# A decode block on one core: short loops on every engine, a model dimension cut in four chunks of 112, and a TensorE program that is walked over once before it runs

## The chip, the cores and the metric

The kernel runs on one core of a Trainium2 chip. The metric is the device time in microseconds of that core, from launch to end; the kernel before has a median of 1302.09 us over 3 runs (1301.49 to 1303.19). The profiler gives one further execution, with the time of every instruction and of every DMA packet.

## The reference, cut to what matters

Everything is fp32. One token (Sq = 1) for B = 2 batches goes through one attention block over a cache of 8192 keys and values per head, and one gated feed-forward block.

```python
B, D, H, Sk, Dh, F = 2, 448, 16, 8192, 256, 1792
x = A_x                                             # [2, 1, 448]
q = (layernorm(x) @ wq).reshape(B, 1, H, Dh)        # wq [448, 4096]
scores = einsum("bhqd,bhkd->bhqk", q, k_cache) * Dh ** -0.5
o = einsum("bhqk,bhkd->bhqd", softmax(scores), v_cache)
h = x + o.reshape(B, 1, H * Dh) @ wo                # wo [4096, 448]
n = layernorm(h)
return h + ((n @ w_gate) * (n @ w_up)) @ w_down     # [448, 1792] twice, [1792, 448]
```

Keys and values are 2 x 16 x 8192 x 256 numbers each, 268 MB and 268 MB; the weights add 24 MB.

## The kernel before, in words

There are 32 pairs of head and batch, numbered i = 0 to 31 (`NQ`). For each pair, K(i) is one load of 8 MB into one of two SBUF buffers (`k_sb[i % 2]`, 128 partitions by 64 keys by 256) and V(i) one load of 8 MB into a single buffer `v_sb`. SP issues all loads but x, in the order of its program; its DMA queue works them off in that order. After K(0) and K(1) come V(0), K(2), V(1), K(3) and so on. SP waits before each: K(i+1) is issued when VectorE is done with K(i-1) (`m_in[i-1]`), V(i) when TensorE has mixed V(i-1) (`pe("M", i-1)`), and V(0), which lies where the weight wq lay, when all queries are projected (`all_q`).

VectorE multiplies K(i) in place with the query, spread over the 128 partitions (`score`, L334), and adds up each key's 256 products (L337): first the 16 keys per partition of `HC`, then the other 48. Between them it does small steps of the pair before (`neg_max` L343, `norm` L348). TensorE (`find_top` L422, `spread_top` L426, `add_up` L431, `spread_query` L270, `mix` L413, `turn_up` L438) finds the maximum, sums the exponentials, spreads the next query and mixes V(i) in 32 matmuls. ScalarE does the exponentials and the copies out of PSUM. An fp32 matmul stands in the profile as two MATMUL records and two LDWEIGHTS records.

Only TensorE's program has a loop, over 31 of the 32 pairs, in which its waits compare a semaphore with a number worked out from the loop's register (`emit_part`). VectorE, ScalarE and SP have every pair written out. After the loop TensorE's program goes on with the last pair, the output projection, and the feed-forward block.

The model dimension of 448 is cut as three chunks of 128 rows and one of 64. The 64 rows of the last chunk lie in two halves of the 128 partitions: its left columns on partitions 0 to 63, its right columns on partitions 64 to 127 (`pack`, `LAYOUT`). So wq, w_gate and w_up are loaded as 128 partitions of 3.5 x 4096, 3.5 x 1792 and 3.5 x 1792 numbers, with no hole. `LAYOUT` needs a fifth slot in `xz` and `xr`, filled with zeros where the other half's rows would be.

At the end, SP issues wo (two loads, behind `m_in[30]`), V(31) in two parts of 48 and 16 keys per partition (`LASTV`), wg (w_gate) and wu (w_up, two loads) behind `m_in[31]`, and wd (w_down, four loads of `DOWN` = 5, 5, 3 and 1 blocks) behind the mix of V(31)'s first part (`mixed_a`). The last steps are the matmuls with wd (L738), a copy (L747) and the store of the output.

Of the kernel before, what the change touches and what calls it, by code (L numbers as in the profile page):

```python
# [9 lines left out]
EPS = 1e-5  # L10
P = 128
HALF = 64
DC = 4
YN, YW = 4, D // 4
# [7 lines left out]
LASTV = 48  # L22

FG = (512, 512, 384, 384)
FO = (0, 512, 1024, 1408)
NF = F // P
FH = FG[0] // 2
WIDE = [[min(n, (k + 1) * FH) - k * FH for n in FG] for k in range(2)]
PACKED = [3 * sum(n) + n[0] + n[2] for n in WIDE]
# [3 lines left out]
LAYOUT = (  # L33
    (slice(0, P), slice(0, DC - 1), slice(0, DC - 1)),
    (slice(0, HALF), slice(DC - 1, DC), slice(DC - 1, DC)),
    (slice(HALF, P), slice(DC - 1, DC), slice(DC, DC + 1)),
)


class Line:  # L40


    def __init__(self, nc, engine, name):
        self.e = engine
        self.sem = nc.alloc_semaphore(name=name)
        self.n = 0
        self.seen = {}

    def wait(self, *tokens):
        for sem, n in tokens:  # L50
            if self.seen.get(sem.num, 0) < n:
                self.e.wait_ge(sem, n)
                self.seen[sem.num] = n

    def did(self, ins):
        ins.then_inc(self.sem, 1)
        self.n += 1
        return self.sem, self.n


class Tensor:


    def __init__(self, nc):
        self.e = nc.tensor
        self.sem = nc.alloc_semaphore(name="pe")
        self.n = 0
        self.parts = [(None, [])]

    def loop(self, *turns):  # L70

        self.parts.append((turns or None, []))

    def do(self, make, *waits, inc=False):
        self.parts[-1][1].append((make, waits, inc))
        if inc:
            self.n += 1
            return self.sem, self.n

    def emit(self):  # L80
        for turns, ops in self.parts:
            if turns:
                with self.e.Fori(*turns) as turn:
                    self.emit_part(ops, turn)
            else:
                self.emit_part(ops, None)

    def emit_part(self, ops, turn):
        seen = {}
        for make, waits, inc in ops:  # L90
            for w in waits:
                sem, n = w[:2]
                if len(w) == 3:
                    self.e.wait_ge(sem, turn * w[2] + n)
                elif seen.get(sem.num, 0) < n:
                    self.e.wait_ge(sem, n)
                    seen[sem.num] = n
            ins = make() if turn is None else make(turn)
            if inc:
                ins.then_inc(self.sem, 1)  # L100


def decode_block(nc, x, k_cache, v_cache, wq, wo, wg, wu, wd, out):
# [6 lines left out]
    bank = [nc.alloc_psum_tensor(f"bank{i}", [P, 512], F32)[:] for i in range(8)]  # L110
    first_sem = nc.alloc_semaphore(name="dve_first")
    V = Line(nc, nc.vector, "dve")
    A = Line(nc, nc.scalar, "act")
    A_q = Line(nc, nc.scalar, "act_q")
    G = Line(nc, nc.gpsimd, "pool")
    S = Line(nc, nc.sync, "sp")
    T = Tensor(nc)

# [3 lines left out]
    def load(line, dst, src, sem, n=16):  # L122
        line.e.dma_start(dst, src).then_inc(sem, 16)  # L123
        return sem, n
# [5 lines left out]

    room = {"at": 2 * NF * D}

    def late(*shape):

        n = 1
        for k in shape[1:]:
            n *= k
        at = room["at"]
        room["at"] += -(-n // 8) * 8
        assert room["at"] <= NJ * DH  # L140
        got = k_flat[1][: shape[0], at : at + n]
# [15 lines left out]
    xr = sb("xr", P, DC + 1, B, 16)  # L157
    xz = sb("xz", P, DC + 1, B)
    sel = sb("sel", P, 2)
    rep = sb("rep", P, 2, B, REP)  # L160
    q_sb = sb("q_all", B, H * DH)

    s_x, s_wq, s_k0 = landing("x"), landing("wq"), landing("k0")
    s_k = [landing("k_even"), landing("k_odd")]
    s_v, s_v2 = landing("v"), landing("v_last")
    s_wo = [landing("wo_a"), landing("wo_b")]
    s_wg, s_wu = landing("wg"), [landing("wu_a"), landing("wu_b")]
    s_wd = [landing(f"wd{i}") for i in range(len(DOWN))]
    s_out = landing("out")
# [7 lines left out]
    x_in = load(A, x_sb, x.rearrange("b s d -> (b s) d"), s_x)  # L177
    wq_t = v_flat[:, : 3 * H * DH + H * DH // 2]
    wq_in = load(S, wq_t, wq, s_wq)
    k0_in = load(S, k_sb[0][:, :HC], keys_of(k_cache, 0, 0, HC), s_k0)  # L180
    k_in = {0: load(S, k_sb[0][:, HC:], keys_of(k_cache, 0, HC, NJ), s_k[0])}
    k_in[1] = load(S, k_sb[1], keys_of(k_cache, 1, 0, NJ), s_k[1])

    zero = G.did(nc.gpsimd.memset(ident, 0.0))
    G.wait(zero)
    ident_in = G.did(
        nc.gpsimd.affine_select(
            out=ident, in_=ident, compare_op=ALU.not_equal, fill=1.0, base=0,
            pattern=[[-1, P]], channel_multiplier=1,
        )  # L190
    )
    G.did(nc.gpsimd.memset(xz, 0.0))
    zeros_in = G.did(nc.gpsimd.memset(xr[:, DC - 1 :], 0.0))

    V.did(nc.vector.memset(eps_t, EPS))
    V.did(nc.vector.memset(ones, 1.0))
    V.did(nc.vector.memset(avg, 1.0 / D))
    V.did(nc.vector.memset(row, DH**-0.5))
    o_ps, h_ps, y_ps = bank[0], bank[5][:, :P], bank[6][:, :YW]
    V.wait(x_in)  # L200
    xsum = sb("xsum", B, 1)
    t = V.did(nc.vector.tensor_reduce(xsum, x_sb, axis=AX.X, op=ALU.add))
    V.wait(t)
    xmean = sb("xmean", B, 1)
    t = V.did(nc.vector.tensor_scalar(xmean, xsum, -1.0 / D, None, op0=ALU.mult))
    V.wait(t)
    xc_sb = sb("xc", B, DC * P)
    t = V.did(nc.vector.tensor_scalar(xc_sb[:, :D], x_sb, xmean, None, op0=ALU.add))
    V.wait(t)
    xc_in = V.did(nc.vector.tensor_copy(xc_sb[:, D:], xc_sb[:, D - HALF : D]))  # L210
    xq = o_sb[:B, :D]
    t = V.did(nc.vector.tensor_mul(xq, xc_sb[:, :D], xc_sb[:, :D]))
    V.wait(t)
    xvar = sb("xvar", B, 1)
    var_in = V.did(nc.vector.tensor_reduce(xvar, xq, axis=AX.X, op=ALU.add))

    std = sb("std", B, 1)
    A.wait(var_in)
    std_in = A.did(nc.scalar.activation(std, xvar, AF.Sqrt, bias=eps_t, scale=1.0 / D))
    rstd = sb("rstd", B, 1)  # L220
    V.wait(std_in)
    rstd_in = V.did(nc.vector.reciprocal(rstd, std))
    A.wait(rstd_in)
    A.did(nc.scalar.activation(std, std, AF.Exp, scale=0.0))

    xT_ps = bank[3][:, : DC * B].rearrange("p (c b) -> p c b", b=B)
    for c in range(DC):
        xT_in = T.do(
            lambda c=c: nc.tensor.transpose(
                xT_ps[:, c, :], xc_sb[:, c * P : (c + 1) * P], ident[:B, :B]  # L230
            ),
            ident_in, xc_in, inc=c == DC - 1,
        )
    V.wait(xT_in, zeros_in)
    for rows, c, to in LAYOUT:
        xz_in = V.did(nc.vector.tensor_copy(xz[rows, to], xT_ps[rows, c]))

    V.wait(ident_in)
    V.did(
        nc.vector.tensor_reduce(  # L240
            sel, ident.rearrange("p (g r) -> p r g", r=32)[:, :2, :], axis=AX.X, op=ALU.add
        )
    )
    V.did(
        nc.vector.tensor_copy(
# [4 lines left out]
    for ps in (o_ps, h_ps, bank[4][:, :HW]):  # L250
        set_in = V.did(nc.vector.memset(ps, 0.0))

    q_sel = sb("q_sel", B, DH)
    qb = [sb(f"qb{i}", P, DH) for i in range(2)]
    qb_ps = bank[1][:, :DH]
    q_ps = [bank[7][:B, :], bank[4][:B, :]]
    qsel_in, qb_in, Q_in = {}, {}, {}

    def select(i):
        h, b = divmod(i % NQ, B)  # L260
        if i > 0:
            A.wait(Q_in[i - 1])
        qsel_in[i] = A_q.did(
            nc.scalar.activation(  # L264
                q_sel, q_sb[:, h * DH : (h + 1) * DH], AF.Copy, scale=ident[:B, b : b + 1]
            )
        )

    def spread_query(*_):
        return nc.tensor.matmul(qb_ps, ones[:B, :], q_sel, start=True, stop=True)  # L270

    def take_query(i):
        A.wait(Q_in[i])
        qb_in[i] = A_q.did(nc.scalar.activation(qb[i % 2], qb_ps, AF.Copy))  # L274

    q_in = {}
    for g in range(NG):
        for c in range(DC):
            xs = c if c < DC - 1 else c + g // (NG // 2)
            at = c * H * DH + (g * QG if c < DC - 1 else g % (NG // 2) * QG)  # L280
            done = T.do(
# [536 lines left out]
```

## Time and profile before

| what | before |
|---|---|
| median of 3 runs | 1302.09 us (1301.49 to 1303.19) |
| profiled execution, its own time | 1301.42 us |
| its span, first to last instruction | 1300.1 us |
| VectorE busy | 1131.2 us (87%) |
| TensorE matmuls busy | 470.6 us (36%) |
| ScalarE busy | 81.5 us (6%) |
| DMA from HBM | 561.19 MB, mean 432 GB/s over the span |
| share of the span in which the SP queue's packets keep 16 DMA engines | 99.7% |

The page gives busy time per engine, the span in 40 slices, the DMA queues, the chain of work that ended last, and the costliest groups of instructions. Busy shares say which engine could be the bound; the wait in front of an instruction, with what released it, says which is.

### The profile page before, as it was taken

The numbers are of one execution on the slowest core, as the hardware profiler recorded it, in microseconds if no ns is written. First come the engines' busy times: TensorE is split into PE (matmuls) and PEld (weight loads), VectorE is DVE, ScalarE is ACT, GpSimd is POOL, SyncE is SP. The second block draws the span as 40 slices with busy tenths as digits, with TensorE's granted clock in tenths as the row PEclk, the third lists the DMA queues.
The fourth block names the chain that finished last, engine by engine and source line by source line (L and its number), as shares of the span: only waits on it lengthen the run. The fifth ranks groups of instructions, "written<-read, shape, count | busy, mean of one in ns | idle before, by whom it ended". The sixth has DMA issues, their size and how long they took to land.

```text
span 1300.1 us, 6914 instructions
## 1 busy us (share of the span) xinstructions
PE 470.6 (36%) x2992; PEld 155.1 (12%) x2992; DVE 1131.2 (87%) x266; ACT 81.5 (6%) x239; POOL 0.8 (0%) x8
## 2 busy tenths in 40 slices
PE   3643224333323433322333322333321333432387
PEld 0111011101001101101101101101100110110123
DVE  1999998889888889888889988888988888988861
ACT  1100000000000000000000000000000000000000
POOL 0000000000000000000000000000000000000000
PEclk9866566666556666556666656666656666655689
DMA  9999999999999999999999999999999999999998
GB/s 411 427 450 421 450 421 444 426 436 436 421 450 421 448 423 448 423 446 425 442 427 427 444 421 450 422 446 425 446 423 446 425 440 429 427 444 423 446 421 367
DMA packets 10973, 561.31 MB, mean 432 GB/s; under 512 B 1234, under 2 KB 1364, under 8 KB 1492
## 3 DMA queue, kind: packets, MB, share of 16 engines
q1 hardware_dynamic: 10960, 561.19, 99.7%
q8 instruction: 5, 0.08, 0.0%
q14 instruction: 4, 0.03, 0.0%
q10 hardware_dynamic: 4, 0.00, 0.0%
HBM read 561.19 MB, written 0.00 MB: 432 GB/s over the span
## 4 chain that ended last, share of the span: by engine, by line
DMA 74%; PE 25%; issue 0%; ACT 0%; SPq 0%; DVE 0%
DMA v<-in_A_v_cache_dram 71%; PE bank L413 22%; PE bank L282 2%; DMA v<-in_wd_dram 2%; DMA v<-in_wq_dram 1%; PE bank L270 0%; SPq L123 0%; PE bank L738 0%; ACT q_all L290 0%; ACT q_sel L264 0%; DVE k L747 0%; ACT qb L274 0%
## 5 line engine op out<-in xcount | busy, mean ns | idle before, releaser
L334 DVE TENSOR_TENSOR k<-k,qb 128x4096 f32<-128x4096 f32 x64 | 555.3, 8676 | 124.2 <-DMA k<-in_A_k_cache_dram 95.9
L337 DVE TENSOR_REDUCE s<-k 128x16 f32<-128x4096 f32 x64 | 555.2, 8675 | 1.1
L413 PE MATMUL bank<-v,p 128*2 128x512 f32 x2048 | 291.4, 733 | 342.9 <-DMA v<-in_A_v_cache_dram 342.9
L413 PEld LDWEIGHTS bank<-v,p 128*2 128x2 f32 x2048 | 53.6, 96 | 573.4 <-DMA v<-in_A_v_cache_dram 365.9
L426 PE MATMUL bank<-nm,row 1*128 1x1 f32 x64 | 18.4, 354 | 227.6 <-DVE nm L343 227.6
L422 PE MATMUL bank<-ident,m 128*1 128x128 f32 x32 | 11.8, 368 | 184.4 <-DVE m L381 184.4
L363 ACT ACTIVATE o_sb<-bank 128x512 f32<-128x512 f32 x31 | 18.5, 597 | 604.0 <-PE bank L413 604.0
L426 PEld LDWEIGHTS bank<-nm,row 1*128 1x128 f32 x64 | 15.6, 302 | 236.9 <-DVE nm L343 236.9
L438 PE MATMUL bank<-sel,o_sb 128*128 128x1 f32 x256 | 33.7, 253 | 23.3 <-ACT o_sb L363 22.5
L270 PE MATMUL bank<-q_sel,ones 2*128 2x256 f32 x66 | 39.0, 691 | 1.4 <-ACT q_sel L264 1.4
L438 PEld LDWEIGHTS bank<-sel,o_sb 128*128 128x128 f32 x256 | 31.0, 191 | 53.1 <-ACT o_sb L363 51.5
L282 PE MATMUL bank<-v,xz 128*2 128x512 f32 x64 | 30.7, 639 | 16.0 <-DMA v<-in_wq_dram 16.0
L352 ACT ACTIVATE nb<-bank 128x1 f32<-128x1 f32 x32 | 5.5, 171 | 441.5 <-PE bank L426 441.5
L431 PE MATMUL bank<-lsum,ones 128*128 128x1 f32 x64 | 18.5, 359 | 23.5 <-ACT p L355 23.5
L422 PEld LDWEIGHTS bank<-ident,m 128*1 128x1 f32 x32 | 2.5, 79 | 188.2 <-DVE m L381 187.8
L431 PEld LDWEIGHTS bank<-lsum,ones 128*128 128x128 f32 x64 | 15.8, 306 | 26.2 <-ACT p L355 26.2
L270 PEld LDWEIGHTS bank<-q_sel,ones 2*128 2x128 f32 x66 | 15.9, 297 | 3.7 <-ACT q_sel L264 2.4
L264 ACT ACTIVATE q_sel<-q_all,ident 2x256 f32<-2x256 f32 x33 | 16.2, 492 | 0.0
L274 ACT ACTIVATE qb<-bank 128x256 f32<-128x256 f32 x32 | 12.2, 382 | 54.5 <-PE bank L270 54.5
L493 PE MATMUL bank<-k,oT 128*2 128x224 f32 x120 | 13.4, 387 | 0.0
L343 DVE TENSOR_REDUCE nm<-bank 1x1 f32<-1x128 f32 x32 | 8.7, 272 | 4.4 <-PE bank L422 4.4
L597 DVE TENSOR_REDUCE k<-bank 128x1 f32<-128x128 f32 x1 | 0.3, 292 | 13.1 <-PE bank L589 13.1
(81 smaller groups left out, 97.3 us busy)
## 6 DMA issues: line engine op xcount, KB each, us to landing
v<-in_wq_dram SPq DMA_DIRECT2D x1, 7168.0 KB, 19.5
k<-in_wo_dram SPq DMA_DIRECT2D x2, 3584.0 KB, 35.3
k<-in_A_k_cache_dram SPq DMA_DIRECT2D x1, 6144.0 KB, 38.0
v<-in_A_v_cache_dram SPq DMA_DIRECT2D x1, 6144.0 KB, 21.6
k<-in_wg_dram SPq DMA_DIRECT2D x1, 3136.0 KB, 28.0
v<-in_wd_dram SPq DMA_DIRECT2D x2, 1120.0 KB, 18.0
k<-in_A_k_cache_dram SPq DMA_DIRECT2D x1, 2048.0 KB, 23.9
v<-in_A_v_cache_dram SPq DMA_DIRECT2D x1, 2048.0 KB, 26.1
```

Of the source, the lines that this page charges most:

```text
L264: nc.scalar.activation(q_sel, q_sb[:, h * DH : (h + 1) * DH], AF.Copy, scale=ident[:B, b : b + 1])
L270: return nc.tensor.matmul(qb_ps, ones[:B, :], q_sel, start=True, stop=True)
L282: lambda g=g, c=c, xs=xs, at=at: nc.tensor.matmul(q_ps[g % 2], xz[:, xs, :], wq_t[:, at : at + QG], start=(c == 0), stop=(c == DC - 1),),
L334: t = V.did(nc.vector.tensor_mul(kt, kt, q[:, None, :].to_broadcast([P, hi - lo, DH])))
L337: V.did(nc.vector.tensor_reduce(s_t[i % 2][:, lo:hi], kt, axis=AX.X, op=ALU.add)),
L363: osb_in[i] = A.did(nc.scalar.activation(o_sb, o_ps, AF.Copy))
L413: lambda *_, t=t, g=g: nc.tensor.matmul(o_ps[g : g + 2, :], p_t[:, 2 * t : 2 * t + 2], v_sb[:, 2 * t : 2 * t + 2, :], start=(t < 4), stop= ...
L422: return T.do(lambda *_: nc.tensor.transpose(mT_ps, m_t, ident), m, inc=True)
L426: lambda *_: nc.tensor.matmul(nb_ps, row, nm, start=True, stop=True), nm_done, inc=True
L431: lambda *_: nc.tensor.matmul(l_ps, ones, lsum, start=True, stop=True), p_done, inc=True
L438: lambda *_, c=c, k=k: nc.tensor.matmul(oT_ps[:, c : c + 1], o_sb[:, (2 * k + c) * P : (2 * k + c + 1) * P], sel[:, k : k + 1], start=(k = ...
L493: lambda h=h, c=c, k=k: nc.tensor.matmul(acc_ps[HALF * k : HALF * k + B, :], oT[:, h, c, :], wo_c[:, h, c, k * HW : (k + 1) * HW], start=F ...
```

## The change

It does the following; the diff is cut to its core.

- A class `Engine` records the program of each of the five engines and writes it out at the end. `roll` makes a loop on the chip, in which each wait is worked out from the loop's register; `only` puts instructions of one turn behind a branch. VectorE runs pairs 1 to 30 as 15 turns of two, ScalarE all 32 as 16 turns of two, TensorE all 32 as 32 turns, and the query projection as 4 turns of two groups. SP's loads stay written out.
- TensorE's program is cut in three (`cut`) and stands in a loop of two passes. Each part is behind a branch that passes it by in the first pass.
- The model dimension is cut in four chunks of 112 (`W`), so wq, wg and wu lie on 112 partitions with 4/3.5 of the row length, and `LAYOUT`, the fifth slot and the zero fills go.
- V(31) comes in three parts of 40, 16 and 8 (`LAST`), wg in two loads; wd waits for the whole mix of V(31), no longer for the first part. The last head's output projection goes into the same sum `acc` as the others; one ScalarE copy of it also adds up the mean.
- The groups of gate and up columns are 512, 512, 512 and 256 wide, before 512, 512, 384 and 384.
- Between turns 0 and 1 of the query projection stands only the first spread of a query; the second is behind all projections.

```diff
+    def emit(self, known):
+        if not self.cuts:
+            self.emit_ops(self.items, known, {})
+            return
+        seen, at = {}, [0, *self.cuts, len(self.items)]
+        with self.nc.Fori(0, 2, 1, engines=[self.e.engine]) as go:
+            for lo, hi in zip(at, at[1:]):
+                with self.e.If(go > 0):
+                    self.emit_ops(self.items[lo:hi], known, seen)
...
+    def emit_turn(self, turns, steps, turn, known, seen):
...
+                self.e.wait_ge(sem, turn * a + b if a else b)
...
-    wq_t = v_flat[:, : 3 * H * DH + H * DH // 2]
+    wq_t = v_flat[:W, : DC * H * DH]
+    wg_t = k_flat[1][:W, : DC * F]
+    wu_t = k_flat[1][:W, DC * F : 2 * DC * F]
...
+    for k, n in enumerate(LAST):
+        load(S, v_sb[:, at : at + n], keys_of(v_cache, NQ - 1, at, at + n), ...
+             ("M", NQ - 2), ...)
+    for k, part in enumerate((slice(0, GC), slice(GC, DC * F))):
+        load(S, wg_t[:, part], wg[:, part], landing(f"wg{k}"), ("wg", k), ("m", NQ - 1))
+    for k, n in enumerate(DOWN):
+        load(S, v_flat[:, at * D : (at + n) * D], wd[:, at * D : (at + n) * D],
+             landing(f"wd{k}"), ("wd", k), ("M", NQ - 1))
...
+    def project_groups(t):
+        for k in range(2):
+            for c in range(DC):
+                T.do(lambda turn, k=k, c=c: nc.tensor.matmul(q_ps[k], xz[:, c, :],
+                        wq_t[:, bass.ds(turn * (2 * QG) + (c * H * DH + k * QG), QG)], ...),
+                    *([("q", 2 * (t - 1) + k)] if c == 0 else []), ...)
+        T.only(t == 0, spread_query, 0, "Q0")
+    T.roll(0, NG // 2, 1, project_groups)
+    spread_query(1)
...
+    V.roll(1, NQ - 1, 2, lambda i: (scores(i), scores(i + 1)))
+    A.roll(0, H, 1, act_turn)
+    T.roll(0, NQ, 1, tensor_turn)      # with T.only(last, heads_out, k): wo for heads 0-7, 8-14
+    T.cut()
+    project_out(H - 1, H, ("oT", NQ - 1), done="acc")
+    A.do(lambda: nc.scalar.activation(sums, acc_ps, AF.Copy, accum_out=total), "acc", done="sums")
...
+    project(u_ps[0], wu_t[:, halves[0]], WIDE[0], lambda c: [("wu", 0)], ("u", 0))
+    T.cut()
...
+    def rows(a, order=range(DC)):                       # in pack
+        a = a.reshape(DC, W, -1)[list(order)]
+        return a.transpose(1, 0, 2).reshape(W, -1)
```

More of the change, by code (lines that the diff above doesn't have):

```diff
@@ L40 @@
[L40 to L84, printed above, removed]
-            else:
[L86 to L100, printed above, removed]
@@ L108, in big, with load @@
         return nc.alloc_sbuf_tensor(name, list(shape), F32, align_bytes=256)[:]
[L110 to L117, printed above, removed]
     def landing(name):
         return nc.alloc_semaphore(name=name)
-    def load(line, dst, src, sem, n=16):
-        line.e.dma_start(dst, src).then_inc(sem, 16)
-        return sem, n
+    bank = [nc.alloc_psum_tensor(f"bank{i}", [P, 512], F32)[:] for i in range(8)]
+    known = {}
+    first_sem = landing("none")
+    V, A, G, S, T = (
+        Engine(nc, *engine)
+        for engine in (
+            (nc.vector, "dve"), (nc.scalar, "act", ("qsel", "qb"), ("q",)), (nc.gpsimd, "pool"),
+            (nc.sync, "sp"), (nc.tensor, "pe", ("qp", "Q0")),
+        )
+    )
+    def load(line, dst, src, sem, name, *waits, n=16):
+        line.do(lambda: line.e.dma_start(dst, src).then_inc(sem, 16), *waits)
+        known[name] = sem, n
     k_sb = [big(f"k{i}", P, NJ, DH) for i in range(2)]
@@ new lines, in decode_block @@
+    load_k(0, lo=HC)
+    load_k(1)
+    for i in range(NQ):
+        if 2 <= i + 1 < NQ:
+            load_k(i + 1, ("m", i - 1))
+        if i < NQ - 1:
+            load(
+                S, v_sb, keys_of(v_cache, i, 0, NJ), s_v, ("v", i),
+                "all_q" if i == 0 else ("M", i - 1), n=16 * (i + 1),
+            )
+    cut = H * D
+    for k in range(2):
+        part = slice(k * cut, (k + 1) * cut)
+        load(S, wo_t[:, part], wo[:, part], landing(f"wo{k}"), ("wo", k), ("m", NQ - 2))
@@ L193, in decode_block @@
[L193 to L245, printed above, removed]
+        ),
+        "zero", done="ident",
+    )
+    for t, value in ((eps_t, EPS), (ones, 1.0), (avg, 1.0 / D), (row, DH**-0.5)):
+        V.do(lambda t=t, value=value: nc.vector.memset(t, value))
@@ new lines, in spread_query @@
+    def spread_query(i, name="Q"):
+        T.do(
+            lambda *_: nc.tensor.matmul(qb_ps, ones[:B, :], q_sel, start=True, stop=True),
+            ("qsel", i), done=(name, i),
+        )
+    def project_groups(t):
+        for k in range(2):
+            for c in range(DC):
+                T.do(
+                    lambda turn, k=k, c=c: nc.tensor.matmul(
+                        q_ps[k], xz[:, c, :],
+                        wq_t[:, bass.ds(turn * (2 * QG) + (c * H * DH + k * QG), QG)],
+                        start=(c == 0), stop=(c == DC - 1),
+                    ),
+                    *([("q", 2 * (t - 1) + k)] if c == 0 else []),
+                    done=("qp", 2 * t + k) if c == DC - 1 else None,
+                )
+        T.only(t == 0, spread_query, 0, "Q0")
@@ L402, in every, with collect @@
-    def every(tokens):
-        sem, n = tokens[0]
-        by = tokens[1][1] - n
-        assert all(tokens[i] == (sem, n + by * i) for i in range(TURNS)), tokens
-        return sem, n, by
-    def mix(lo, hi, landed):
+            ),
+            ("nb", i), done=("p", i),
+        )
+    def collect(i, turn_of):
+        b = i % B
+        A.do(lambda *_: nc.scalar.activation(o_sb, o_ps, AF.Copy), ("M", i), done=("osb", i))
+        A.do(
+            lambda turn: nc.scalar.activation(
+                oT[:, bass.ds(turn_of(turn), 1), :, b], oT_ps[:, None, :], AF.Copy, scale=rl
+            ),
+            ("O", i), ("rl", i), done=("oT", i),
+        )
@@ L434, in turn_up, with project_out @@
-    def turn_up(o_done):
+    def project_out(lo, hi, *waits, done=None):
+        for h in range(lo, hi):
+            for c in range(2):
+                for k in range(2):
+                    last = h == hi - 1 and c == k == 1
+                    T.do(
+                        lambda h=h, c=c, k=k: nc.tensor.matmul(
+                            acc_ps[HALF * k : HALF * k + B, :], oT[:, h, c, :],
+                            wo_c[:, h, c, k * HW : (k + 1) * HW],
+                            start=False, stop=(h == H - 1 and c == 1),
+                        ),
+                        *(waits if h == lo and c == k == 0 else []), done=done if last else None,
+                    )
@@ new lines, in heads_out, with hold @@
+    def heads_out(k):
+        if k == 0:
+            for j in range(2):
+                T.do(
+                    lambda j=j: nc.tensor.matmul(
+                        acc_ps[HALF * j : HALF * j + B, :], ident[:B, :B],
+                        x_sb[:, j * HW : (j + 1) * HW], start=True, stop=False,
+                    )
+                )
+            project_out(0, H // 2, ("wo", 0), ("oT", H - 1))
+        else:
+            project_out(H // 2, H - 1, ("wo", 1), ("oT", NQ - 3))
+    def hold(*waits):
+        T.do(None, *waits)
@@ new lines, in tensor_turn @@
+    def tensor_turn(i):
+        last = i == NQ - 1
+        T.only(last, heads_out, 0)
+        T.do(
+            lambda *_: nc.tensor.transpose(mT_ps, m_t, ident), ("m", i), done=("T", i)
+        )
+        T.do(
+            lambda *_: nc.tensor.matmul(nb_ps, row, nm, start=True, stop=True),
+            ("nm", i), done=("N", i),
+        )
+        T.do(
+            lambda *_: nc.tensor.matmul(l_ps, ones, lsum, start=True, stop=True),
+            ("p", i), done=("L", i),
+        )
+        spread_query(i + 2)
+        T.only(last, heads_out, 1)
+        at = 0
+        for k, n in enumerate(LAST):
+            if k > 0:
+                T.only(last, hold, ("v_last", k))
+            mix(
+                i, at, at + n, *([("v", i)] if k == 0 else []),
+                done=("M", i) if k == len(LAST) - 1 else None,
+            )
+            at += n
@@ L647, in decode_block @@
[L647 to L674 removed]
+                    *([("osb", i)] if c == k == 0 else []),
@@ new lines, in tensor_turn @@
+                    done=("O", i) if c == k == 1 else None,
+                )
+    T.roll(0, NQ, 1, tensor_turn)
+    T.cut()
+    project_out(H - 1, H, ("oT", NQ - 1), done="acc")
+    sums, total, mean = late(P, HW), late(P, 1), late(P, DC, B)
+    A.do(
+        lambda: nc.scalar.activation(sums, acc_ps, AF.Copy, accum_out=total), "acc", done="sums"
+    )
+    for j in range(2):
+        T.do(
+            lambda j=j: nc.tensor.matmul(
+                xc_ps[:, 2 * j : 2 * j + 2, :], sums[:, j * W : (j + 1) * W],
+                ident.rearrange("p (k r) -> p k r", k=2)[:, :, :B], start=(j == 0), stop=False,
+            ),
+            "sums",
+        )
@@ new lines, in decode_block @@
+    V.do(
+        lambda: nc.vector.tensor_mul(mean, share, total[:, None, :].to_broadcast([P, DC, B])),
+        "sums", "share", done="mean",
+    )
+    T.do(
+        lambda: nc.tensor.matmul(xc_ps, ones[:, :W], mean, start=False, stop=True),
+        "mean", done="xc_h",
+    )
+    for q in range(DC):
+        T.do(
+            lambda q=q: nc.tensor.matmul(
+                y_ps[32 * q : 32 * q + 32, :], rep[:, q // 2].rearrange("p b r -> p (b r)"),
+                sums[:, q % 2 * W : (q % 2 + 1) * W], start=True, stop=False,
+            )
+        )
@@ new lines, in decode_block, with project @@
+    V.do(
+        lambda: nc.vector.tensor_copy(sr, sq_sum[:, None, :, None].to_broadcast([W, 4, B, REP])),
+        "sq_sum", done="sr",
+    )
+    V.do(lambda: nc.vector.tensor_scalar_add(ve, var, EPS), "var", done="ve")
+    V.do(lambda: nc.vector.reciprocal(rv, ve), "ve", done="rv")
+    V.do(
+        lambda: nc.vector.memset(u_ps[1][3 * 32 :, :], 0.0), ("osb", NQ - 1), done="u_blank"
+    )
+    def project(ps, w, wide, landed, done, between=None):
+        for c in range(DC):
+            at = c * sum(wide)
+            for g, n in enumerate(wide):
+                if n > 0:
+                    T.do(
+                        lambda c=c, g=g, n=n, at=at: nc.tensor.matmul(
+                            ps[32 * g : 32 * g + 32, :n], xr[:, c].rearrange("p b r -> p (b r)"),
+                            w[:, at : at + n], start=(c == 0), stop=(c == DC - 1),
+                        ),
+                        *landed(c), done=done if c == DC - 1 and at + n == DC * sum(wide) else None,
+                    )
+                at += n
```

787 lines of the change are left out of this document (335 added, 452 removed).

## The prediction

> **What bounds the kernel now.** I read the page first: busy shares, the slices of DMA, the queues.
>
> ```profile
> span 1300.1 us, 6914 instructions
> PE 470.6 (36%) x2992; PEld 155.1 (12%) x2992; DVE 1131.2 (87%) x266; ACT 81.5 (6%) x239; POOL 0.8 (0%) x8
> ...
> DMA packets 10973, 561.31 MB, mean 432 GB/s; under 512 B 1234, under 2 KB 1364, under 8 KB 1492
> ## 3 DMA queue, kind: packets, MB, share of 16 engines
> q1 hardware_dynamic: 10960, 561.19, 99.7%
> q8 instruction: 5, 0.08, 0.0%
> q14 instruction: 4, 0.03, 0.0%
> ```
>
> SP's queue keeps the 16 DMA engines 99.7% of the span: the stream of loads is the bound, and no byte of it goes. A change can only alter its rate, open a gap in it, or move its two ends. The stages of windows show those ends (columns: stretch, length, busy time and count of PE, PEld, DVE, ACT, POOL, granted clock, DMA share, GB/s).
>
> ```profile
> 1.00:2.00 1.00, 0.00 (x0) 0.00 (x0) 0.16 (x3) 0.69 (x1) 0.42 (x3) 1.00 2.55 806
> ...
> 1294.00:1295.00 1.00, 0.52 (x24) 0.28 (x12) 0.00 (x0) 0.00 (x0) 0.00 (x0) 1.00 0.93 384
> 1295.00:1296.00 1.00, 0.67 (x28) 0.68 (x32) 0.00 (x0) 0.00 (x0) 0.00 (x0) 1.00 0.69 274
> 1296.00:1297.00 1.00, 0.54 (x26) 0.30 (x19) 0.00 (x0) 0.00 (x0) 0.00 (x0) 1.00 0.29 113
> 1297.00:1298.00 1.00, 0.93 (x32) 0.67 (x32) 0.00 (x1) 0.00 (x0) 0.00 (x0) 1.00 0.01 4
> ```
>
> The stream begins in the second microsecond and is empty by 1297. In between it isn't empty all at once: the share falls 0.93, 0.69, 0.29, so some of the 16 engines end two microseconds behind others. Were all level, the last would end earlier by the sum of what is missing, 0.07 + 0.31 + 0.71 = 1.1 us. The timeline shows what follows the last landings.
>
> ```profile
> 1295.33 1.17 PE L738 MATMUL bank<-v,k 128*32 128x112 f32 x40 [0.81 <-DMA v<-in_wd_dram]
> 1296.95 0.97 PE L738 MATMUL bank<-v,k 128*32 128x112 f32 x32 [0.46 <-DMA v<-in_wd_dram]
> ...
> 1298.00 0.28 DVE L747 COPY k<-bank 128x112 f32<-128x112 f32 x1 [4.11 <-PE bank L738]
> 1298.30 0.72 SPq L123 DMA_DIRECT2D out_dram<-k  x1
> ```
>
> TensorE still waits 0.81 and 0.46 us for parts of wd, then 3.15 us (1296.95 to 1300.1) go into matmuls, copy and store. So the end is: last wd landing plus 3.15 us.
>
> **The change part by part.** First the loads that go from 128 partitions to 112; the table of DMA issues gives their sizes and times to landing.
>
> ```profile
> v<-in_wq_dram SPq DMA_DIRECT2D x1, 7168.0 KB, 19.5
> k<-in_A_k_cache_dram SPq DMA_DIRECT2D x1, 6144.0 KB, 38.0
> k<-in_wg_dram SPq DMA_DIRECT2D x1, 3136.0 KB, 28.0
> k<-in_A_k_cache_dram SPq DMA_DIRECT2D x1, 2048.0 KB, 23.9
> k<-in_wu_dram SPq DMA_DIRECT2D x1, 1792.0 KB, 31.9
> k<-in_wu_dram SPq DMA_DIRECT2D x1, 1344.0 KB, 34.6
> ```
>
> Bytes stay: 4 x 112 = 3.5 x 128 = 448 rows. At 432 GB/s, wq's 7168 KB (7.34 MB) are 17.0 us, wg's 3136 KB (3.21 MB) 7.43 us, wu's 1792 + 1344 = 3136 KB another 7.43: 31.9 us together. The stream's rate is known only for loads that fill 128 partitions; the trace has none of size on fewer. Lower end: every DMA engine carries 7 of 112 rows that are 8/7 as long, and writes them as fast: 0. If instead the rate goes with the partitions that are written at one time, 112/128 of it, each of these loads takes 8/7 as long: 31.9 / 7 = +4.55 us (wq 2.43, wg 1.06, wu 1.06). Upper end: sevens that start anywhere straddle the old eights, and in some of the time two engines write to one place at half rate; estimate for two of seven rows: 2/7 x 31.9 = +9.1, and twice that, 18, if wq and its followers also get in each other's way. I take +4.55: it scales the one rate that the rows show with the one thing that changes, while 0 needs 112 partitions to take what 128 took at full stretch. Since the stream never pauses, nothing gives this back.
>
> [...]
>
> **The front.** The queue must not run dry before V(0) is issued.
>
> ```profile
> 0.73 0.39 SPq L123 DMA_DIRECT2D v<-in_wq_dram  x1
> ...
> 20.32 9.78 PE L282 MATMUL bank<-v,xz 128*2 128x512 f32 x16 [16.02 <-DMA v<-in_wq_dram]
> 30.03 0.69 PE L270 MATMUL bank<-q_sel,ones 2*128 2x256 f32 x2
> 30.65 3.59 PE L282 MATMUL bank<-v,xz 128*2 128x512 f32 x8
> 35.68 0.69 PE L270 MATMUL bank<-q_sel,ones 2*128 2x256 f32 x2 [1.43 <-ACT q_sel L264]
> 36.30 17.33 PE L282 MATMUL bank<-v,xz 128*2 128x512 f32 x40
> 53.66 0.33 SPq L123 DMA_DIRECT2D v<-in_A_v_cache_dram  x1
> ```
>
> Queued at first are 7168 + 2048 + 6144 KB and K(1)'s 8192, together 24.1 MB or 55.8 us; begun at 1.8 (806 GB/s in the second window counts packets that start there), they last to 57.6. V(0) is issued at 53.66 and needs about 1.0 (wq: issue 0.73, stream 1.8), so slack is 2.9 us. After: wq lands 2.43 later; the projections stay 64 records, less the wait of 1.43 and the second spread's 0.69 that now stand behind them: V(0) issued at 53.66 + 2.43 - 2.12 = 54.0, while the queue also ends 2.43 later. Cost 0; slack grows to 5.0.
>
> The first pass over TensorE's program costs its sequencer three skipped parts and a jump back. It lies where TensorE idles 16.02 us for wq. Its bounds are 0 (a few branches) and whatever exceeds that idle time plus 5.0 us of slack; I take 0. The later parts' instructions then come in early. In before, 9 fetches of 0.11 MB run beside the stream, about 12 KB each, on one engine's share of 432 / 16 = 27 GB/s: 0.45 us of one engine's time apiece. Those during the last stage put engines behind, part of the 1.1 us of unevenness. Gain between 0 (early fetches leave an engine behind just as well) and 1.1; I take 0.6, the middle, since rows tell neither.
>
> **The steady part.** Loops give VectorE, ScalarE and TensorE waits worked out from registers. VectorE is the engine to fear.
>
> ```profile
> 1215.64 0.22 DVE L381 TENSOR_REDUCE m<-s 128x1 f32<-128x64 f32 x1
> 1219.40 4.43 DVE L334 TENSOR_TENSOR k<-k,qb 128x4096 f32<-128x4096 f32 x1 [3.54 <-DMA k<-in_A_k_cache_dram]
> 1223.74 0.27 DVE L343 TENSOR_REDUCE nm<-bank 1x1 f32<-1x128 f32 x1
> 1224.06 0.58 PE L426 MATMUL bank<-nm,row 1*128 1x1 f32 x2 [7.78 <-DVE nm L343]
> ...
> 1258.92 0.28 DVE L343 TENSOR_REDUCE nm<-bank 1x1 f32<-1x128 f32 x1 [4.41 <-PE bank L422]
> 1259.25 0.38 PE L426 MATMUL bank<-nm,row 1*128 1x1 f32 x2 [0.37 <-DVE nm L343]
> ```
>
> It waits 3.54 us per pair for K. TensorE's wait on a register starts L426 at 1224.06, 0.05 after nm's end at 1224.01; the wait on a constant of the last pair, 1259.25 against 1259.20, also 0.05. So a computed wait costs 0 beyond noise, against 3.54 us of cover; with that gone, each 0.1 us would cost 0.1 x 30 pairs. ScalarE is busy 6%. TensorE's branch past the last pair's work lies in its long waits.
>
> **The end.** V(31) in three parts lets its mix end sooner after the landing; wd now waits for all of it.
>
> ```profile
> 1275.74 2.21 SPq L123 DMA_DIRECT2D v<-in_wd_dram  x4
> 1277.46 0.60 ACT L560 ACTIVATE o_sb<-bank 128x512 f32<-128x512 f32 x1 [17.15 <-PE bank L413]
> ...
> 1282.59 3.29 PE L668 MATMUL bank<-k,xr 128*32 128x512 f32 x16 [1.22 <-DVE k L643]
> ...
> 1290.01 0.57 PEld L668 LDWEIGHTS bank<-k,xr 128*32 128x32 f32 x16 [0.36 <-DMA k<-in_wu_dram]
> ```
>
> wd would be issued about 1277.4 instead of 1275.74, four issues in 2.21 us to 1279.6; until wu's last landing at 1290.0 the queue is full, so 10 us cover it: 0. Behind SP's wait stand only wd and the store, which come later anyway. Two more loads (V(31)'s third part, wg's second) are two issues of SP, which sits idle: 0. The new way from the last head to the gate (four 224-wide matmuls, one ScalarE copy with its sum, three small matmuls, one VectorE product, one copy for xr in place of three) has no more links than before, where the gate began at 1282.59; a delay up to 0.46 us, TensorE's last wait for wd, is hidden, and above it counts in full; I take 0. Gate and up stay as long as their widest group, 512 and 256 columns.
>
> **Sum.** Profiled execution 1301.42 (span 1300.1 plus 1.32) + 4.55 - 0.6 = 1305.4; the median shown is 0.67 above that execution: 1306.0.
>
> **Rivals.**
> - *The partial loads stream at full rate.* For it: equal bytes, 7 rows to each of 16 engines, the same packet count per engine to within one in eight. Against: a stream at 99.7% leaves no reserve. Then only the ends remain: 1302.1 - 0.6 = 1301.5 (1301.0 to 1302.1), no change, where I forecast slower. It decides as soon as the loads cost under 3.2 us. [...]
> - *Engines collide.* The upper end above, +9.1 to +18 less 0.6: 1310.6 to 1319.5, about 1311. For it: sevens fit no eights; against: no row shows two loads slowing each other.
> - *The first pass comes too late.* If a fetch stood in the queue as loads do (19.5 to 38.0 us to landing), TensorE would miss wq's landing, V(0) would be late and the stream would pause: one pass of 38 us from 0.8 is 38.8 - 22.7 - 5.0 = 11 us over, 1302.1 + 4.55 + 11 = 1318. Against: fetches are not in SP's queue.
> - *Faster by over 0.2%.* Would need 2.6 us, more than all the unevenness; some unseen rate must rise.
> - *VectorE becomes the bound.* Needs over 3.54 us more per pair; 1 us beyond that is +30 us. The 0.05 rows speak against.
>
> **How the numbers follow.** Forecast (partial rate) 0.38; full rate 0.34; collisions 0.16; late pass 0.05; VectorE 0.03; faster 0.04. About 0.2% (2.6 us) is what a measurement of this kernel can tell from no change. Slower: 0.38 + 0.16 + 0.05 + 0.03 = 0.62; same 0.34; faster 0.04. The likeliest gives 1306.0, its own range 1305 to 1308 by 0 to 1.1 of evenness and some microseconds of collision. The range for 8 in 10 takes in the full rate at its best, 1301.0 less 0.2, and the near collisions up to 1314.
>
> **What would show it.** wq's time to landing: about 22 us if the partial rate holds, 19.5 at full rate, 24 or more with collisions; wg's and wu's landings about 1 us further apart each. V(0) issued near 54. Instruction fetches early, none at the end; the last windows less stepped. VectorE's wait for K still some 3.5 us per pair. The prediction is wrong if wq lands in 19.5 us, if V(0)'s issue passes 60, or if the first TensorE matmul on wq starts well after its landing.

## The result and the profile after

| | before | after |
|---|---|---|
| median of 5 runs | 1302.09 us (1301.49 to 1303.19) | 1331.55 us (1330.25 to 1333.79) |
| span of the profiled execution | 1300.1 us | 1328.9 us |
| ratio, 95% interval | | 1.0226 (1.0212 to 1.0240) |

The change makes the kernel 2.3% slower, 29 us where 4 were forecast. One run of the dense version below, at 1339.9 us with a granted clock of 0.53 where all its other runs have 0.64, is a slow one and is left out of that version's ratio, though not of its median. The page of after: the span, the busy times, the slices of DMA, the queues.

```profile
span 1328.9 us, 7597 instructions
PE 481.5 (36%) x2952; PEld 159.0 (12%) x2952; DVE 1129.7 (85%) x255; ACT 83.5 (6%) x245; POOL 0.7 (0%) x6
...
DMA  9999999999999999999999999999999999999998
GB/s 235 441 430 440 440 426 430 440 440 426 432 438 442 424 432 438 442 426 432 436 442 428 432 434 442 432 432 430 442 434 430 430 442 436 430 430 440 424 373 222
DMA packets 11178, 561.27 MB, mean 422 GB/s; under 512 B 1266, under 2 KB 1396, under 8 KB 1524
q1 hardware_dynamic: 11168, 561.19, 99.6%
q8 instruction: 3, 0.05, 0.0%
```

and the same two rows of slices of before:

```profile
DMA  9999999999999999999999999999999999999998
GB/s 411 427 450 421 450 421 444 426 436 436 421 450 421 448 423 448 423 446 425 442 427 427 444 421 450 422 446 425 446 423 446 425 440 429 427 444 423 446 421 367
```

The bytes are the same and the queue is as full as before (99.6%, before 99.7%). No gap opened. But GB/s in the first slice is 235 (before 411) and in the last two 373 and 222 (before 421 and 367), while the DMA row has the same digits in both kernels: 9, and 8 in the last slice. The loss lies in two places, and the busy share hides it. Stretches of the windows (stretch, length, busy time and count of PE, PEld, DVE, ACT, POOL, granted clock, DMA share, GB/s), of after:

```profile
4.00:30.00 26.00, 0.50 (x4) 0.45 (x4) 1.87 (x8) 1.87 (x4) 0.00 (x0) 1.00 0.99 244
80.00:1240.00 1160.00, 389.56 (x2377) 128.13 (x2377) 1060.42 (x215) 67.93 (x213) 0.00 (x0) 0.61 1.00 434
1286.00:1318.00 32.00, 18.75 (x126) 7.28 (x129) 2.10 (x10) 2.00 (x5) 0.00 (x0) 0.68 1.01 245
```

and the same reading of before, at wq and in the steady part:

```profile
4.00:18.00 14.00, 0.30 (x3) 0.21 (x2) 2.34 (x11) 1.78 (x3) 0.00 (x0) 1.00 1.06 459
80.00:1240.00 1160.00, 386.03 (x2374) 126.30 (x2370) 1062.07 (x211) 66.54 (x208) 0.00 (x0) 0.61 1.00 434
```

The 1160 us in the middle run at 434 GB/s in both. While wq streams (4 to 30), and again while wg and wu do (1286 to 1318), the same 16 busy engines move 244 and 245 GB/s. In these stretches the three weights arrive whose loads went from 128 partitions to 112. (GB/s counts the packets that start in a stretch, so a short one can be some per cent off.) The timeline and the DMA issues of after give the places:

```profile
67.22 0.33 SPq L167 DMA_DIRECT2D v<-in_A_v_cache_dram  x1
19.39 0.50 PE L328 MATMUL bank<-ident,xc 2*112 2x2 f32 x4 [19.39 <-issue]
35.69 10.18 PE L361 MATMUL bank<-v,xz 112*2 x16 [15.80 <-DMA v<-in_wq_dram]
...
1232.84 4.42 DVE L420 TENSOR_TENSOR k<-k,qb 128x4096 f32<-128x4096 f32 x1 [3.48 <-DMA k<-in_A_k_cache_dram]
...
1317.72 1.06 PE L649 MATMUL bank<-k,xr 112*32 112x256 f32 x12 [2.11 <-DMA k<-in_wu_dram]
1321.80 0.69 PE L682 MATMUL bank<-ident,k 128*128 128x128 f32 x2 [0.54 <-DVE k L677]
1322.42 4.36 PE L703 MATMUL bank<-v,k 128*32 128x112 f32 x112
1326.85 0.28 DVE L712 COPY k<-bank 128x112 f32<-128x112 f32 x1 [3.90 <-PE bank L703]
1327.16 0.71 SPq L167 DMA_DIRECT2D out_dram<-k  x1
...
v<-in_wq_dram SPq DMA_DIRECT2D x1, 34.6
```

Against the prediction's rows of before, the delay grows in three steps:

| point | before | after | late by |
|---|---|---|---|
| first projection with wq | 20.32 | 35.69 | 15.4 |
| VectorE takes the last K it waits for, late in the steady part | 1219.40 | 1232.84 | 13.4 |
| TensorE takes wu's last part | 1290.01 | 1317.72 | 27.7 |
| end of the span | 1300.1 | 1328.9 | 28.8 |

So wq costs 13.4 us that stay, the end's loads another 14.3, and what follows wu's last landing 1.1 (11.2 us, before 10.1). In before TensorE waited for wd at the very end; here wd has mostly landed before its matmuls can begin, and all 112 run in one block of 4.36 us, 39 ns apart, where before 40 took 1.17, 29 ns apart. The granted clock differs with the pace:

```profile
1322.00:1327.00 5.00, 4.78 (x114) 4.20 (x113) 0.57 (x2) 0.00 (x0) 0.00 (x0) 0.65 0.14 56
```

It is 0.65 there, and was 1.00 in before's last microseconds.

### The profile page after: what moved, and what is told of

The parts are those of the page before. It is cut to its first block, busy times and chain, and to the rows that moved or that the text cites. A ratio compares the mean times of both kernels' runs of the same rounds, so it can differ in the third digit from the quotient of the medians.

```text
span 1328.9 us, 7597 instructions
## 1 busy us (share of the span) xinstructions
PE 481.5 (36%) x2952; PEld 159.0 (12%) x2952; DVE 1129.7 (85%) x255; ACT 83.5 (6%) x245; POOL 0.7 (0%) x6
## 3 DMA queue, kind: packets, MB, share of 16 engines
q1 hardware_dynamic: 11168, 561.19, 99.6%
## 4 chain that ended last, share of the span: by engine, by line
DMA 50%; DVE 40%; issue 8%; PE 1%; DVEq 0%; ACT 0%; SPq 0%
DMA k<-in_A_k_cache_dram 44%; DVE s L429 21%; DVE k L420 18%; DMA k<-in_wu_dram 4%; DMA v<-in_wq_dram 3%; PE bank L361 1%; PE bank L703 0%; DVE m L442 0%; PE bank L649 0%; DVE nm L448 0%; DVE rl L453 0%; DVEq L140 0%; PE bank L682 0%; SPq L167 0%; ACT q_all L377 0%
## 5 line engine op out<-in xcount | busy, mean ns | idle before, releaser
L551 PE MATMUL bank<-ident,m 128*1 128x128 f32 x32 | 11.8, 369 | 177.8 <-DVE m L442 177.8
L554 PEld LDWEIGHTS bank<-nm,row 1*128 1x128 f32 x64 | 15.6, 301 | 238.6 <-DVE nm L448 238.6
L353 PE MATMUL bank<-q_sel,ones 2*128 2x256 f32 x68 | 39.8, 684 | 0.0
L361 PE MATMUL bank<-v,xz 112*2 x64 | 30.9, 646 | 15.8 <-DMA v<-in_wq_dram 15.8
L388 ACT ACTIVATE q_sel<-q_all,ident 2x256 f32 (+1 forms) x35 | 17.2, 493 | 0.0
L522 PE MATMUL bank<-k,oT 128*2 128x224 f32 x128 | 16.6, 428 | 0.5 <-ACT oT L486 0.5
L649 PE MATMUL bank<-k,xr 112*32 112x256 f32 (+1 forms) x88 | 12.9, 670 | 9.1 <-DMA k<-in_wu_dram 6.9
```

What stands on the lines that cost most here:

```text
L353: lambda *_: nc.tensor.matmul(qb_ps, ones[:B, :], q_sel, start=True, stop=True),
L361: lambda turn, k=k, c=c: nc.tensor.matmul(q_ps[k], xz[:, c, :], wq_t[:, bass.ds(turn * (2 * QG) + (c * H * DH + k * QG), QG)], start=(c == ...
L388: return nc.scalar.activation(q_sel, q_sb[:, bass.ds(at, DH)], AF.Copy, scale=ident[:B, b : b + 1])
L522: lambda h=h, c=c, k=k: nc.tensor.matmul(acc_ps[HALF * k : HALF * k + B, :], oT[:, h, c, :], wo_c[:, h, c, k * HW : (k + 1) * HW], start=F ...
L551: lambda *_: nc.tensor.transpose(mT_ps, m_t, ident), ("m", i), done=("T", i)
L554: lambda *_: nc.tensor.matmul(nb_ps, row, nm, start=True, stop=True),
```

## The experiments

Theory A: a DMA on 112 partitions streams at little over half the rate because of which partitions it fills, whatever else changed. Rival B: it is the row length or the packets that follow from it. Rival C: the loops and the two passes (instruction fetches, a late TensorE) slow the stream. A form of A that only counts rows, and how they are dealt to the engines, is told apart further down.

**After, with the loads on 128 partitions.** 16 rows of zeros are added to wq, wg and wu (2.0 MB in all); all else is after.

```diff
-    load(S, wq_t, wq, ...)
+    load(S, v_flat[:, : DC * H * DH], wq, ...)
+    # wg, wu: k_flat[1][:, ...] likewise; in pack, rows():
+    a = np.concatenate([a, np.zeros((P - W, a.shape[1]), a.dtype)], axis=0)
```

> The changed kernel, but wq, wg and wu are stored with 16 rows of zeros below the 112 and loaded as 128 partitions; nothing that computes changes, and 8/7 of those weights' bytes are moved (2.0 MB more). Theory A (loads on 112 partitions run at half rate, because the engines get in each other's way on the partitions they write): the loads run at the 432 GB/s of the others, wq (8.39 MB) lands near 1.8 + 19.4 + 0.5 = 21.7 us instead of 35.4, and the time falls to 1302.1 + 4.5 = 1306 us, or 0.6 less if the later instruction fetches are gone. Theory B (the longer row length of 65536 bytes slows wq's load; not the rows' number): the loads stay at half rate and the time stays at 1331 us or above. Theory C (the slower part is TensorE's first pass or the loops): 1331 us, give or take 2.

Measured: 1306.03 us (1305.89 to 1306.46), ratio 1.0030 (1.0018 to 1.0041), span 1304.6. Two stretches, the front and the last loads, and rows of the timeline and of the DMA issues:

```profile
4.00:20.00 16.00, 0.51 (x4) 0.45 (x4) 1.90 (x8) 1.87 (x4) 0.00 (x0) 1.00 1.04 450
1277.00:1295.00 18.00, 13.57 (x117) 5.76 (x116) 2.10 (x10) 1.99 (x5) 0.00 (x0) 0.81 1.01 429
...
15.61 0.51 PE L328 MATMUL bank<-ident,xc 2*112 2x2 f32 x4 [15.61 <-issue]
24.32 8.17 PE L361 MATMUL bank<-v,xz 112*2 x14 [8.21 <-DMA v<-in_wq_dram]
...
1297.84 1.17 PE L703 MATMUL bank<-v,k 128*32 128x112 f32 x40
v<-in_wq_dram SPq DMA_DIRECT2D x1, 23.3
```

Loading 2.0 MB more makes the kernel 25 us faster than after. The rows are as long as in after, the passes and loops are the same, and the rate is back at 450 and 429 GB/s. A stands. B falls, since the rows are as long as in after and are moved in packets of the same length (SP's queue has 11248 packets where after has 11168: 16 more, one per row of zeros, for each of the five loads). C can hold no more than a small part: of the 4.1 us that are left above before, the 2.0 MB take 4.6 by the stream's 432 GB/s.

**After, with one pass over TensorE's program.**

```diff
-    T.cut()      # both
```

> The changed kernel with TensorE's program in one pass (both cuts taken out; the loops, the 112-row loads and all else stay). Theory A (112-row loads): no change within 2 us of 1331.5, since the first pass (TensorE's first transposes at 19.4 us instead of 3.7) ends before wq lands at 35.4; the transposes come back to about 3.7 us. Theory C (the first pass delays the front): V(0) is issued sooner than 67.2 us and the time falls by up to 13 us. Instruction fetches come back into the end of the stream under both.

Measured: 1334.13 us (1331.72 to 1334.99), ratio 1.0239 (1.0222 to 1.0256). This is 2.6 us above after, where I had expected no change within 2; the intervals of the two ratios overlap. From its timeline and DMA issues:

```profile
3.78 0.50 PE L328 MATMUL bank<-ident,xc 2*112 2x2 f32 x4 [3.78 <-DVE xc L312]
35.22 9.33 PE L361 MATMUL bank<-v,xz 112*2 x16 [30.94 <-DMA v<-in_wq_dram]
65.89 0.33 SPq L167 DMA_DIRECT2D v<-in_A_v_cache_dram  x1
v<-in_wq_dram SPq DMA_DIRECT2D x1, 34.1
```

TensorE is ready at 3.78 again, 15.6 us earlier than in after, and then waits 30.94 us for the same late wq. So the first pass falls as a cause: it put TensorE's start 15.6 us later, and wq's landing hid that.

**Loads alone, by number of rows.** No block is computed and the output is zeros; nine loads with rows of 64 KB from partition 0 on, one after the other, three more from other partitions on, and three with rows of 16 KB.

```diff
+    for rows in (128, 112, 96, 80, 64, 48, 32, 16, 120):
+        nc.sync.dma_start(to[:rows, :js], src[:rows, :js]).then_inc(sem, 16)
+        nc.sync.wait_ge(sem, 16)
```

> No block is computed: this kernel only loads keys, one load after the other, each waited for, with 65536 bytes per row and 128, 112, 96, 80, 64, 48, 32, 16 and 120 rows from partition 0, then 112 rows from partition 16, 96 from 32 and 64 from 64, then 128, 112 and 96 rows of 16384 bytes; the output is filled with zeros. Theory A (collisions on the partitions written): 128 rows take about 19.4 + 2 us; 112 rows 33 to 35 us (7.3 MB at 220 GB/s); 96 and 80 also below the full rate; 64 rows about half rate (19 us) if they keep only half of the places busy; short rows behave the same (112 rows of 16384 bytes at about 220 GB/s). Theory B (row length): 112 rows of 16384 bytes run at the full rate, and 112 rows of 65536 take no longer than 128 rows of 65536. Forecast's proportional rate: 112, 96, 80 rows each take as long as 128 (19.4 us).

The windows of it, one stretch per load in that order (length, DVE, POOL, clock, DMA share, GB/s); the last two are 128 and 112 rows of 16 KB:

```profile
1.70:22.30 20.60, 0.00 (x0) 0.00 (x0) 1.00 0.97 407
23.50:55.00 31.50, 0.00 (x0) 0.00 (x0) 1.00 0.96 233
56.30:86.50 30.20, 0.00 (x0) 0.00 (x0) 1.00 0.98 208
88.30:114.00 25.70, 0.00 (x0) 0.00 (x0) 1.00 0.96 204
116.10:137.00 20.90, 0.00 (x0) 0.00 (x0) 1.00 0.96 201
138.60:163.90 25.30, 0.00 (x0) 0.00 (x0) 1.00 0.94 124
165.30:176.10 10.80, 0.00 (x0) 0.00 (x0) 1.00 0.92 194
177.50:186.80 9.30, 0.00 (x0) 0.00 (x0) 1.00 0.93 113
189.00:230.20 41.20, 0.00 (x0) 0.00 (x0) 1.00 0.92 191
...
319.30:325.30 6.00, 0.00 (x0) 0.00 (x0) 1.00 0.91 350
326.50:333.60 7.10, 0.00 (x0) 0.00 (x0) 1.00 0.90 258
```

112 rows take 31.5 us (I had expected 33 to 35), 128 rows of the same length 20.6: fewer bytes, half as long again. Only 128 rows reach full rate; 120 rows fall to 191. My proportional rate would have put 112 rows at 356 GB/s. And 64 rows (201) are hardly above 32 (194). Where the block starts changes little: 112 rows from partition 16 on reach 236 GB/s, 96 from 32 on 204, 64 from 64 on 201. With rows a quarter as long 112 rows still fall behind 128 (258 to 350), so long rows aren't needed for it; the loss is smaller there, 0.74 of the rate against 0.57, and I had expected about 220. The single packets, one row each, show the same: with 128 rows most take 2.42 us, and with 112 none of them takes less than 3.06. In after's trace nearly all rows of K and V that are as long as wq's take 2.42, and wq's own 112 take 3.15 or more.

**Before, with wq cut in two loads of 64 partitions.** If A holds, the old kernel can be made slow with none of the change in it.

```diff
-    wq_in = load(S, wq_t, wq, s_wq)
+    load(S, wq_t[:HALF], wq[:HALF], s_wq)
+    wq_in = load(S, wq_t[HALF:], wq[HALF:], s_wq, 32)
```

> The kernel before, with one edit: the load of wq is cut by partitions into two loads of 64 rows (0 to 63, 64 to 127), same bytes, same layout. Theory A: each half keeps only half of the places busy, the load of 7.34 MB takes 34 us instead of 17, wq lands near 37 us instead of 20.2, everything behind it in the queue comes about 15 to 17 us later, and the time rises to about 1318 us. V(0) is then issued at about 70.5 us, before the queue runs dry at about 74. If only the number of rows per engine mattered (4 to each of 16 engines), wq would land within 1 us of 20.2 and the time would stay at 1302.

Measured: 1321.24 us (1320.22 to 1322.71), ratio 1.0148 (1.0131 to 1.0165). The front's window, and its first projection and V(0)'s issue:

```profile
4.00:36.00 32.00, 0.28 (x3) 0.19 (x2) 2.31 (x11) 1.78 (x3) 0.00 (x0) 1.00 0.97 201
...
39.93 9.40 PE L283 MATMUL bank<-v,xz 128*2 128x512 f32 x16 [35.66 <-DMA v<-in_wq_dram]
72.90 0.33 SPq L123 DMA_DIRECT2D v<-in_A_v_cache_dram  x1
```

The halves run at 201 GB/s, the rate of 64 rows measured alone, and one after the other: the landings in the trace have the first half in by 22.0 us and the second by 39.8. The kernel loses 19 us, where I had expected 16; the two halves don't help each other at all.

**The same rows, other partitions.** Again no block is computed and the output is zeros. The step between the partitions written differs, and the loads take turns on three buffers of the same size, two of which hold loads at under 200 GB/s and at over 300.

```diff
+    for rows, step in ((16,1), (16,2), (16,4), (16,8), (32,1), (32,2), (32,4), (64,1), (64,2), (128,1)):
+        nc.sync.dma_start(to[: rows * step : step], src[:rows]).then_inc(sem, 16)
```

> No block is computed: loads of keys only, one after the other, 65536 bytes per row, where the same rows of the key cache go to partitions that lie apart: 16 rows at steps of 1, 2, 4 and 8 partitions, 32 rows at steps of 1, 2 and 4, 64 rows at steps of 1 and 2, then 128; the output is filled with zeros. [...] Theory A2 (any count of rows but 128 is spread badly over the engines, wherever it goes): the step changes nothing, 16 rows take 9.3 us and 32 rows 10.7 us at every step.

Windows in that order, those of 32, 64 and 128 rows (columns as above):

```profile
35.90:46.50 10.60, 0.00 (x0) 0.00 (x0) 1.00 0.94 198
48.40:59.20 10.80, 0.00 (x0) 0.00 (x0) 1.00 0.92 194
61.30:67.60 6.30, 0.00 (x0) 0.00 (x0) 1.00 0.91 333
69.20:90.10 20.90, 0.00 (x0) 0.00 (x0) 1.00 0.96 201
92.00:103.10 11.10, 0.00 (x0) 0.00 (x0) 1.00 0.93 378
104.30:124.90 20.60, 0.00 (x0) 0.00 (x0) 1.00 0.98 407
```

64 rows on partitions 0 to 63 take 20.9 us; the same rows on every second partition of 128 take 11.1. 32 rows go from 10.6 to 6.3 when spread by four. The stretches not shown, of 16 rows, go from 110 GB/s at step 1 to 194, 187 and 191 at steps 2, 4 and 8. The rows, their length, the packets and the source are the same, so the places written set the rate; the count of rows, and how it divides among the engines, can't explain the difference. Of these loads of 32 and 64 rows, those at 194 to 201 GB/s stay within partitions 0 to 63, and those at 333 and 378 span all 128.

**After, 128 rows and one pass.** The first experiment, also without `T.cut()`.

> The kernel of the zero rows (wq, wg and wu on 128 partitions, 112 of them used) with TensorE's program in one pass. If the first pass is worth nothing: 1306 us within 0.6, the first transposes near 3.8 us instead of 15.6. If its early instruction fetches save what the prediction took for them: 0.6 us slower, 1306.6, with fetches after 1260 us and engines that end further apart (1.65 us from first to last with two passes, 1.85 in the kernel before).

Measured: 1306.41 us (1306.11 to 1307.18), ratio 1.0033 (1.0020 to 1.0046), against 1.0030 with two passes. The intervals lie on one another: the two passes are worth nothing that these runs can tell. TensorE's first transposes stand at 3.84 us with one pass and at 15.61 with two, and wq takes 21.8 us to landing against 23.3.

**After, with before's dense layout.** The loops, the passes and the new end stay; `pack`, `LAYOUT`, the fifth slot and the group widths are before's, so that wq, wg and wu lie on 128 partitions with no hole and no more bytes.

```diff
-    wq_t = v_flat[:W, : DC * H * DH]
+    wq_t = v_flat[:, : 3 * H * DH + H * DH // 2]
-    T.roll(0, NG // 2, 1, project_groups)
+    # two rolls of two turns: left columns with zeros in one slot, right in the other
```

> The changed kernel (loops on all engines, TensorE in two passes, the new end) with the layout of the kernel before for wq, wg and wu: three chunks of 128 rows and one of 64 on both halves, 128 partitions, no zero rows, same bytes as before. Theory A (the row count of the loads is all of the loss): 1306.0 - 4.55 = 1301.5 us, at or just under the kernel before (1301.9 to 1302.1); the first pass must end before wq's landing at 20.2 us. Theory C (the rest of the change costs time that the wider loads only hide): above 1304.

Measured: 1301.57 us, before beside it 1301.99; ratio 0.9995 (0.9987 to 1.0004). Its timeline and DMA issues:

```profile
20.95 0.56 PE L338 MATMUL bank<-ident,xc 2*128 2x2 f32 x4 [20.95 <-issue]
23.58 8.44 PE L375 MATMUL bank<-v,xz 128*2 x16 [2.07 <-DVE bank L361]
53.37 0.33 SPq L171 DMA_DIRECT2D v<-in_A_v_cache_dram  x1
v<-in_wq_dram SPq DMA_DIRECT2D x1, 7168.0 KB, 21.0
```

All of the change but the 112 partitions is worth nothing measurable: by the interval, between 1.7 us gained and 0.5 lost. The loss is in the layout. This is also the best version in hand, and it doesn't beat before by more than the interval.

## Why the prediction was wrong

The sign was right, and for the reason given: the loads on 112 partitions are slower, and a full stream gives nothing back. The size was not: 1331.55 lies far above 1306.0 and outside the range. By its steps:

- **The step that failed: the price of the partial loads.** I took 112/128 of the rate, +4.55 us, with 0 and 18 as the ends. The term measures 27.7 us, 13.4 for wq and 14.3 for the end's loads. In after they run at 244 to 245 GB/s, by which their 13.8 MB take about 56 us where the prediction counted 31.9, some +24. Most of the rest is unevenness: by the landings in the traces, the first and the last of the 16 engines land wu's last part 4.6 us apart, in before 1.9. Alone, 112 rows run at 233 against 407 for 128, a ratio of 0.57 and not 0.88.
- **The upper end was an estimate with no row behind it.** The rival of colliding engines came nearest, and wq's 34.6 us to landing is past the 24 that I had named as its sign: the places written set the rate, though that engines meet at them is not shown by itself. I sized it by two of seven rows at half rate, where alone every row of 112 is slower than the 2.42 us that most rows of 128 take. No load of size on fewer than 128 partitions was in the trace, so no rate was there to scale, and a range closed at 18 had no ground. Half rate, +32, was the bound to keep.
- **The rule I used did not hold.** I let the rate go with the share of the 128 partitions that a load fills; no row of before showed that. From the 407 GB/s of 128 rows it gives 356 for 112, 382 for 120 and 204 for 64. The runs have 233 and 191, and the same 64 rows take two values: 201 side by side, and 378 at step 2, where they span the partitions without filling them. That the kernel with 16 rows of zeros lies 4.1 us above before, near my 4.55, is no support for my rule: there the rate is full, and 8/7 of the bytes are moved.
- **The rival of full rate fell** with wq's 34.6 us to landing, against 19.5. Equal bytes for each of 16 engines say nothing of how fast each writes: the DMA share is 0.99 at 244 GB/s, and 1.00 at 434.
- **What held.** The stream is the bound, and bytes and fullness stay. VectorE still waits up to 3.6 us for K, in after's waits:

```profile
DVE k L420 <- DMA k<-in_A_k_cache_dram: 97.1, 28, 3.6
```

  So computed waits cost nothing that shows, and VectorE did not become the bound. V(0) is issued at 67.22, past the 60 that I had named as a sign of error. It is late only because wq is, and nothing ran dry: the steady part is at 434 GB/s.
- **The first pass cost 0, with less margin than I gave it.** TensorE reaches its first transposes at 19.39 instead of about 4. The DMA queue of instructions moves two blocks of 16 KB before that moment, at 6.00 and 15.78, and a third after it, at 23.61; in the dense version three of four come before TensorE's start at 20.95. That these fetches make up the whole delay isn't shown. Under after's late wq it is free. In the dense version wq has landed at 21.8 us by the trace's landings, TensorE's first matmul on it stands at 23.58, and only V(0)'s slack, which I put at 5.0 us, takes that in (issue at 53.37, before 53.66). The stream seems to pay for the fetches too: three of the 16 engines land their share of this wq at 21.5 to 21.8, the other 13 by 20.0, and before's wq is complete at 20.2. I put that down to the three fetches, by their number alone.
- **The early fetches** were priced at -0.6. The dense version is 0.4 us below before, within its interval, and with zero rows the one pass is 0.4 us slower than two; neither shown nor excluded.
- **The end** was priced at 0 and cost 1.1 us, all of it between wu's last landing and the store, where the granted clock is 0.65. With 128 rows the same code takes 10.1 us there again, from 1294.51 to 1304.6, with wd's first 40 matmuls in 1.17 us, so it comes with the slow loads; why the clock falls there wasn't tried.

Open: the exact rule by which the places set the rate. It has to give 407 GB/s for 128 rows, 191 for 120 and 233 for 112, and for 64 rows 201 side by side and 378 at step 2. How the rows are dealt to the engines, and whether engines that write to the same places slow each other, wasn't tried.

## What to carry to other kernels

Where loads bound the kernel, fill all 128 partitions in each, even with zeros: 2 MB of padding bought 25 us here, and a dense layout without the padding another 4.5. Read GB/s by stage beside the busy share, since 16 engines at little over half the rate look as busy as at full (here a share of 0.99 at 244 GB/s and 1.00 at 434). When a trace holds no instance of what a change introduces, keep the range open to the worst that its nearest kin could mean, or measure that one thing by itself first; a kernel of loads alone shows it in 350 us.

## What the runs showed of the hardware that was not expected

- A DMA's rate isn't in proportion to its rows: 407, 191, 233, 208, 204, 201, 124, 194 and 113 GB/s for 128, 120, 112, 96, 80, 64, 48, 32 and 16 neighbouring partitions, with rows of 64 KB. 48 is slower than 32.
- With a step between the partitions, 64 rows reach 378 GB/s and 32 rows 333.
- All these loads show a DMA share of 0.91 to 0.98. The share tells that engines have packets, not how fast these move.
- A first pass that skips all of TensorE's program puts its start 15.6 us later (19.39 against 3.78 with one pass) beside a full queue; with 128 rows 11.8 us (15.61 against 3.84). In after two of the 16 KB instruction fetches lie in that time, at 6.00 and 15.78 us.
